# One core: a score block of the next quarter traced before the old quarter's last transpositions, and a routing with its sums in PSUM

## The chip, the core and the metric

The kernel runs on one core of a Trainium2 chip. The metric is device time in microseconds (us) of one execution, the lower the better. The engines are TensorE (PE in the rows), VectorE (DVE), ScalarE (ACT), GpSimd (POOL) and SyncE (SP, which issues most of the DMAs here); PEld is TensorE's loading of weights.

## What is computed

Three stages stand behind each other, all in fp32 accuracy.

1. Attention with random features, for 4 batches, 8 heads, 576 positions, 64 channels and 128 features. For q and k: `proj = x @ omega.T`, `h = proj - sum(x*x)/2`, `phi = exp(h - max(h))`. Then `kv = phi(k).T @ v`, `z = sum(phi(k))`, `out = phi(q) @ kv / (phi(q) @ z)`.
2. A mixture of 8 experts over the 2304 tokens of width 512: `logits = x @ w_gate`, the expert is the argmax of a row, its gate the softmax value there, and `y = gate * (max(x @ w1[e], 0) @ w2[e])`, with an inner width of 1024.
3. A dense layer: `h = x @ w_in` (512 to 2048), `g = h * sigmoid(1.702 h)`, `out = g @ w_out`.

## The kernel before, in words

**Attention in eight quarters.** A quarter is 4 heads of one batch, so two quarters make a batch. Each quarter has a q part (`qgen`) and a k part (`kgen`), which run beside each other: q of quarter i with k of quarter i + 1. The rows of a quarter are cut into five blocks, four of 128 x 512 score elements and one of half the width. A letter and the block's number say what is done:

- P: the score block (`ph_P`). TensorE makes `pr` (L344 in the first quarters, L350 and L351 with two fp16 halves later), VectorE reduces the maximum over features (L359, into a corner of the PSUM tile `small`), does two small operations with the squares sq (L368) and subtracts (L380), which gives `qp`. In k blocks of the first four quarters the subtraction is left to ScalarE's exponential (L376). `pr` has three buffers.
- X: TensorE transposes `qp` into `tq` (L430), ScalarE takes the exponential into `qpT` (L432).
- N: TensorE's products `num` (L444); VectorE adds the epsilon, inverts and scales into `xn` (L446 to L455).
- R: half of the quarter's `xn` is transposed for the experts: four 128-wide pieces into `tx` (L464) and a 64-wide rest into `small` (L466). ScalarE copies both as `xh` (L469), and VectorE makes the remainder `xl` (L473). There are two R per quarter, R0 and R1, and the corner of `small` for the rest exists once, so the second waits until the first was read.

The order of a quarter's steps is written out by hand in a string, and a list scheduler then orders the instructions of each engine by its own estimate, starting from the order in which the code is traced:

```python
W_Q = 17
W_K = 5
Q_ORDER = "P0 P1 X0 P4 X1 N0 P2 X4 N1 X2 P3 N4 X3 N2 R0 N3 R1"
```

Steps of q, of k and of the routing are merged by weights (17, 5 and 10). q and k of a quarter come by DMA into `m` (two buffers). ScalarE and GpSimd split them into fp16 halves `hl` (L307, L308), SyncE transposes these by DMA into `xT` (L309, three buffers), and GpSimd squares and folds `m` (L267, L272) for `sq` (L274). So the split of a later quarter's k stands on ScalarE among the exponentials and the copies `xh`.

**The routing of a batch** (`route_steps`) runs beside the following quarter. TensorE multiplies the gate weights' two halves with xh and xl into `lT_ps` (L529, L530), 16 rows: 8 experts, once for each half. ScalarE copies them as `lT`. Then come five transpositions into `lg_ps` (L537), two VectorE copies (L542, L543) and the sum of the two halves (L545), which is `lg`, tokens by experts. From it come the row maximum `rm`, the one-hot `oh`, `ex` for the softmax, the counts `ct_ps` by a product with ones (L561), the most frequent expert `es` (L565 to L571), and each token's expert number `ixf` (five `max`, five `max_index`, a cast: L588 to L591). SyncE loads `es` into a register (L604); only then can it issue the loads `st` of that expert's weights (L674), which ScalarE and VectorE or GpSimd split into `wh` and `wl` (L698, L700).

**The experts** (`m_ps`, `w_ps`, L136; `h1h` L732; `h1l` L735; `y` L783) are interleaved with attention as soon as routing 0 is done; until then attention runs alone:

```python
while 0 not in gate_t:
    done_a += next(A)
    tick()
```

Routing 3, the last, has attention behind it. Beside it run the last products of batch 2's experts and, on VectorE, the decoding `z` of output weights of the dense layer (L826 to L901). The dense layer follows (`qa` and others, L1146 and L1249).

Of the kernel before, what the change touches and what calls it, by code (L numbers as in the profile page):

```python
# [8 lines left out]
F32 = mybir.dt.float32  # L9
# [3 lines left out]
U32 = mybir.dt.uint32  # L13
I64 = mybir.dt.int64
ACTF = mybir.ActivationFunctionType
ALU = mybir.AluOpType
AX = mybir.AxisListType
# [5 lines left out]
def kernel(  # L23
# [13 lines left out]
    nc = tc.nc  # L37
    B, H, S, D = q.shape
    M = omega.shape[0]
    E, DM, F1 = w1.shape  # L40
    F2 = w_in.shape[1]
    NT = B * S
    P = 128
    T = 4
    TAIL = S - T * P
# [26 lines left out]
    W_Q = 17  # L72
    W_K = 5
    K_ORDER = (0, 1, 4, 2, 3)
    Q_ORDER = "P0 P1 X0 P4 X1 N0 P2 X4 N1 X2 P3 N4 X3 N2 R0 N3 R1"
    LAG_E = 2
    LAG_X = 1
    LAG_M = 0
# [27 lines left out]
    pp = ctx.enter_context(tc.tile_pool(name="pp", bufs=1, space=PSUM))  # L106
# [34 lines left out]
    ident = const.tile([P, P], F32, name="ident")  # L141
# [3 lines left out]
    iota8 = const.tile([P, E], F32, name="iota8")  # L145
# [26 lines left out]
    def setup_wg():  # L172
        nc.sync.dma_start(out=wg, in_=w_gate.rearrange("(k p) e -> p k e", p=P))
        nc.scalar.activation(out=wgs[:, :, 0], in_=wg, func=ACTF.Copy)
        nc.vector.tensor_tensor(out=wgs[:, :, 1], in0=wg, in1=f32(wgs[:, :, 0]), op=ALU.subtract)
# [7 lines left out]
    QB = H // QH  # L183
    NQ = B * QB
    asked = []
    clock = [0]
    late = []

# [107 lines left out]
    def halves_T(src, i, eng):  # L296
        sides[0] += 1
        if sides[0] <= FPX:
            return turned(src, i)
        if sides[0] - 1 in LO_DVE:  # L300
            eng = nc.vector
        m = src[i]
        hl = att.tile([P, NB, 2, D], F16, tag="hl", name="hl", bufs=2)
        xT = att.tile([P, NB, P], F16, tag="xT", name="xT", bufs=3)
        sq = att.tile([P, NB], F32, tag="sq", name="sq", bufs=3)
        for c in (slice(0, 8), slice(8, NB)) if i < FINE else (slice(0, NB),):
            nc.scalar.activation(out=hl[:, c, 0], in_=m[:, c], func=ACTF.Copy)  # L307
            eng.tensor_tensor(out=hl[:, c, 1], in0=m[:, c], in1=hl[:, c, 0], op=ALU.subtract)  # L308
            XQ.dma_start_transpose(out=xT[:, c], in_=hl[:, c].rearrange("p n a d -> p (n a d)"))  # L309
            square_sum(m, c, sq, FOLD_LATE)  # L310
        src[i] = (xT, sq, False)
# [102 lines left out]
    def qgen(i):  # L414
# [5 lines left out]
        src, kv = q_in.pop(i), kv_t.pop(i)  # L420
        xn = att.tile([P, T + 1, QH, D], F32, tag="xn", name="xn", bufs=1)
        xv = xn.rearrange("p t h d -> p t (h d)")
        qp, qt = {}, {}

        def X(i):
            w = 2 if i < 4 else 1
# [52 lines left out]

        for n, op in enumerate(Q_ORDER.split()):  # L480
            g = int(op[1])
            if op == "R0" and qd == 0:
                while x_done[0] < b - 1:
                    yield None
                xh_t[b] = (moe if b % 2 else xep).tile([P, KD, S], F32R, tag="xh", name="xh", bufs=1)
                xl_t[b] = (moe if b % 2 else xep).tile([P, KD, S], F32R, tag="xl", name="xl", bufs=1)
            if op[0] == "P":
                c = ph_P(i, src, qp, "qp", 3, g)
            else:
                c = {"X": X, "N": N, "R": XT}[op[0]](g)  # L490
            if n == 0 and i + 1 < NQ:
                load_v(i + 1)
            if n == KPRE and i + 2 < NQ:
                load_qk(k, k_in, i + 2, asked[-1] if i == QB + 1 else None)
                halves_T(k_in, i + 2, nc.vector if i + 2 < DVE_LO else nc.gpsimd)
            yield c
# [10 lines left out]


    gate_t, reg_t = {}, {}

    def route(b):
        g = route_steps(b)
# [7 lines left out]
    def route_steps(b):  # L520
# [10 lines left out]
            nc.scalar.activation(out=lT[:, c], in_=lT_ps, func=ACTF.Copy)  # L531
        yield 2.0
        yield 0
        lg_ps = pp.tile([P, T + 1, 2, E], F32, tag="n", name="lg_ps", bufs=1)
        for t in range(T + 1):
            n = P if t < T else TAIL
            nc.tensor.transpose(  # L537
                lg_ps[:n, t].rearrange("p a e -> p (a e)"), lT[:, t * P:t * P + n], ident[:2 * E, :2 * E]
            )
        lg2 = att.tile([P, T + 1, 2, E], F32, tag="lg2", name="lg2", bufs=1)  # L540
        nc.vector.memset(lg2[:, T], 0.0)
        nc.vector.tensor_copy(lg2[:, 0:T], lg_ps[:, 0:T])  # L542
        nc.vector.tensor_copy(lg2[:TAIL, T], lg_ps[:TAIL, T])  # L543
        lg = att.tile([P, T + 1, E], F32, tag="lg", name="lg", bufs=1)
        nc.vector.tensor_tensor(out=lg, in0=lg2[:, :, 0], in1=lg2[:, :, 1], op=ALU.add)  # L545


        rm = att.tile([P, T + 1, 1], F32, tag="rm", name="rm", bufs=2)
        nc.vector.tensor_reduce(out=rm, in_=lg, axis=AX.X, op=ALU.max)
# [32 lines left out]
                )  # L582
        cif = att.tile([P, 1], F32, tag="cif", name="cif", bufs=2)
        nc.vector.tensor_copy(cif, ci[:, 0:1])
        mx = att.tile([P, T + 1, 8], F32, tag="lmx", name="lmx", bufs=1)
        ix = att.tile([P, T + 1, 8], U32, tag="lix", name="lix", bufs=1)
        for t in range(T + 1):
            nc.vector.max(mx[:, t], lg[:, t])  # L588
            nc.vector.max_index(ix[:, t], mx[:, t], lg[:, t])
        ixf = att.tile([P, T + 1, 1], F32, tag="ixf", name="ixf", bufs=1)  # L590
        nc.vector.tensor_copy(ixf, ix[:, :, 0:1])  # L591
        eq = att.tile([P, T + 1, 1], F32, tag="eq", name="eq", bufs=1)
        nc.vector.tensor_scalar(out=eq, in0=ixf, scalar1=cif[:, 0:1], scalar2=None, op0=ALU.is_equal)
        nc.vector.memset(eq[TAIL:, T, :], 0.0)
# [405 lines left out]
    if True:  # L1000
# [6 lines left out]
        halves_T(q_in, 0, nc.vector if DVE_LO else nc.gpsimd)  # L1007
        load_qk(k, k_in, 1)
        setup_wg()
        halves_T(k_in, 1, nc.vector if DVE_LO else nc.gpsimd)  # L1010
        A, Mg = attention_gen(), moe_all()
        done_a = done_m = 0.0
# [14 lines left out]
        while a_live:  # L1027
            if force == "a" or (force is None and done_a - lead <= A_RATIO * done_m):
                c = next(A, "end")
# [515 lines left out]
```

## Time and profile before

| what | value |
|---|---|
| median of 3 runs | 767.19 us (766.09 to 768.16) |
| profiled execution | 767.65 us, of which its span 765.6 us |
| TensorE busy | 739.7 us (97%) |
| VectorE busy | 531.3 us (69%) |
| ScalarE busy | 338.6 us (44%) |
| GpSimd busy | 131.9 us (17%) |
| mean granted clock of TensorE | 0.99 |

The span is the time from the first to the last instruction; the execution's time holds some 2 us more. Busy shares are means over stages with different limits: where TensorE is full, the other engines' work lies beside it, and only where TensorE waits do they count. The granted clock is the share of TensorE's full speed.

### The profile page before, as it was taken

The numbers are of one execution on the slowest core, as the hardware profiler recorded it, in microseconds if no ns is written. First come the engines' busy times: TensorE is split into PE (matmuls) and PEld (weight loads), VectorE is DVE, ScalarE is ACT, GpSimd is POOL, SyncE is SP. The second block draws the span as 40 slices with busy tenths as digits, with TensorE's granted clock in tenths as the row PEclk, the third lists the DMA queues.
The fourth block names the chain that finished last, engine by engine and source line by source line (L and its number), as shares of the span: only waits on it lengthen the run. The fifth ranks groups of instructions, "written<-read, shape, count | busy, mean of one in ns | idle before, by whom it ended". The sixth has DMA issues, their size and how long they took to land.

```text
span 765.6 us, 14359 instructions
## 1 busy us (share of the span) xinstructions
PE 739.7 (97%) x5559; PEld 716.1 (94%) x5559; DVE 531.3 (69%) x1188; ACT 338.6 (44%) x638; POOL 131.9 (17%) x78
## 2 busy tenths in 40 slices
PE   7998799999999999989999999999999999999997
PEld 6877699999999999979999999999999999999996
DVE  5867867586776685556879559981368777777774
ACT  5554464335522332233427464554576433444331
POOL 3563377609500441000000000000000000000000
PEclk9999799999999999999999999999999999999999
DMA  5447594456725554198145558972978544443311
GB/s 157 117 131 187 123 302 97 120 140 193 189 60 162 150 179 134 51 234 287 59 161 197 177 171 295 316 263 100 332 273 298 172 138 138 137 129 117 115 29 32
DMA packets 136715, 127.57 MB, mean 167 GB/s; under 512 B 58176, under 2 KB 120896, under 8 KB 135744
## 3 DMA queue, kind: packets, MB, share of 16 engines
q1 hardware_dynamic: 123936, 98.85, 43.5%
q10 hardware_dynamic: 12704, 27.73, 10.3%
q8 instruction: 45, 0.74, 0.4%
q14 instruction: 30, 0.25, 0.1%
HBM read 79.68 MB, written 40.40 MB: 157 GB/s over the span
## 4 chain that ended last, share of the span: by engine, by line
PE 83%; DVE 8%; DMA 4%; issue 1%; ACT 1%; SPq 1%; POOL 0%; ACTq 0%; POOLq 0%; DVEq 0%
PE m_ps L136 19%; PE qa L1249 13%; PE qa L1146 13%; PE qm L1249 7%; PE w_ps L136 4%; PE pb L1249 3%; PE qm L1146 3%; PE qu L1146 3%; PE num L444 3%; PE kv_ps L402 3%; DMA st<-in_moe_w_dram 2%; PE qn L1146 2%; PE qt L1146 2%; PE tq L430 1%; PE pr L344 1%
## 5 line engine op out<-in xcount | busy, mean ns | idle before, releaser
L1146 PE MATMUL qa<-y,wi 128*128 128x384 f32 x576 | 109.2, 337 | 0.4 <-DVE g L901 0.4
L1146 PEld LDWEIGHTS qa<-y,wi 128*128 128x128 f32 x576 | 101.4, 188 | 0.8 <-DVE g L901 0.8
L136 PE MATMUL m_ps<-xh,wh 128*128 128x288 f32 x256 | 79.0, 309 | 4.1 <-DVE h1l L735 2.3
L136 PE MATMUL m_ps<-xh,wl 128*128 128x288 f32 x256 | 76.8, 300 | 0.1
L136 PE MATMUL m_ps<-xl,wh 128*128 128x288 f32 x256 | 76.4, 298 | 0.0
L700 POOL TENSOR_TENSOR wl<-st,wh 128x1024 fp32r<-128x1024 f32 x23 | 55.1, 2401 | 83.0 <-ACT wh L698 82.9
L359 DVE TENSOR_REDUCE small<-pr 128x4 f32<-128x512 f32 (+1 forms) x80 | 51.1, 639 | 11.8 <-PE pr L351 7.8
L698 ACT ACTIVATE wh<-st 128x1024 fp32r<-128x1024 f32 (+1 forms) x33 | 34.0, 1035 | 48.5 <-DMA st<-in_moe_w_dram 31.6
L136 PEld LDWEIGHTS m_ps<-xh,wh 128*128 128x128 f32 x256 | 48.6, 190 | 5.8 <-DVE h1l L735 3.6
L136 PE MATMUL m_ps<-h1h,wh 128*128 128x288 f32 x160 | 48.8, 305 | 0.9 <-DVE h1l L735 0.9
L136 PEld LDWEIGHTS m_ps<-xh,wl 128*128 128x128 f32 x256 | 48.6, 190 | 0.5 <-DVE wl L700 0.4
L735 DVE SCALAR_TENSOR_TENSOR h1l<-m_ps,h1h 128x288 fp32r<-128x288 f32 x64 | 28.9, 453 | 28.9 <-ACT h1h L732 28.8
L136 PEld LDWEIGHTS m_ps<-xl,wh 128*128 128x128 f32 x256 | 48.6, 190 | 0.0
L136 PE MATMUL m_ps<-h1l,wh 128*128 128x288 f32 x160 | 47.7, 298 | 0.0
L136 PE MATMUL m_ps<-h1h,wl 128*128 128x288 f32 x160 | 47.4, 298 | 0.0
L732 ACT ACTIVATE h1h<-m_ps 128x288 fp32r<-128x288 f32 x64 | 25.9, 407 | 48.5 <-PE m_ps L136 46.7
L1249 PE MATMUL qa<-p,p 128*128 128x256 f32 x360 | 46.2, 282 | 1.1 <-DVE p L855 0.8
L1249 PE MATMUL qa<-p,gs 128*128 128x256 f32 x360 | 45.9, 282 | 0.0
L1249 PEld LDWEIGHTS qa<-p,p 128*128 128x128 f32 x360 | 44.2, 189 | 1.6 <-DVE p L855 1.0
L1249 PEld LDWEIGHTS qa<-p,gs 128*128 128x128 f32 x360 | 44.2, 189 | 0.0
L444 PEld LDWEIGHTS num<-kv,qpT 128*128 128x128 f32 (+1 forms) x320 | 36.7, 184 | 5.4 <-ACT qpT L432 3.1
L444 PE MATMUL num<-kv,qpT 128*128 128x65 f32 (+1 forms) x320 | 39.3, 266 | 2.5 <-ACT qpT L432 1.4
(213 smaller groups left out, 1819.5 us busy)
## 6 DMA issues: line engine op xcount, KB each, us to landing
g_dram<-g ACTq DMA_DIRECT2D x48, 384.0 KB, 4.1
st<-in_moe_w_dram SPq DMA_DIRECT2D x31, 512.0 KB, 5.2
pg<-g_dram SPq DMA_DIRECT2D x10, 1024.0 KB, 5.7
raw<-in_moe_w_in_dram SPq DMA_DIRECT2D x16, 512.0 KB, 4.0
gt<-g_dram SPq DMA_DIRECT2D x8, 1024.0 KB, 5.4
p<-wo_dram SPq DMA_DIRECT2D x6, 1024.0 KB, 7.3
yt<-y_dram SPq DMA_DIRECT2D x12, 384.0 KB, 6.0
vm<-in_v_dram SPq DMA_DIRECT2D x32, 128.0 KB, 3.2
```

The lines of the kernel that those rows point to most:

```text
L136: ins = nc.tensor.matmul(out=ps, lhsT=a, rhs=b, start=start and n == 0, stop=stop and n == 2)
L344: nc.tensor.matmul(out=ps[:, :, h2], lhsT=xT[:, (2 * pr + h2) * 2 + t0 // 2], rhs=wbd)
L359: nc.vector.tensor_reduce(out=pm, in_=ps[:, :w], axis=AX.X, op=ALU.max, negate=on_act)
L402: nc.tensor.matmul(out=kv_ps[:, h, :], lhsT=kp[j // 2][:, j % 2, h2, :], rhs=vm[:, h, t, :], start=(t == 0), stop=False,)
L430: nc.tensor.transpose(tq[:, c, h2], qp[i][:, c, h2, :], ident)
L444: nc.tensor.matmul(out=ps[:n, c, h2, :], lhsT=lhsT, rhs=kv[:, h, :])
L698: nc.scalar.activation(out=hi[:, :, s], in_=st[:, :, s], func=ACTF.Copy)
L700: eng.tensor_tensor(out=lo[:, :, s], in0=st[:, :, s], in1=f32(hi)[:, :, s], op=ALU.subtract)
L732: nc.scalar.activation(out=hh[:, f], in_=ps, func=ACTF.Relu)
L735: nc.vector.scalar_tensor_tensor(out=hl[:, f], in0=ps, scalar=0.0, in1=f32(hh[:, f]), op0=ALU.max, op1=ALU.subtract)
L1146: ins = nc.tensor.matmul(out=ps, lhsT=w[:, a, ks], rhs=y[:, b, kk], start=start and kk + m == 0, stop=kk == 1 and m == 2, skip_group_check ...
L1249: ins = nc.tensor.matmul(out=ps, lhsT=x[:, f], rhs=w[i][:, f], start=start and f + m == 0, stop=f == NP - 1 and m == 2, skip_group_check=True,
```

## The change

Three edits. First, the string of steps gets an "F0" in front of R0: the next quarter's block P0 is traced there, and that quarter's own P0 then does nothing. Second, the logits' two halves are summed by TensorE: five fp32 products with a 16 x 8 matrix `fold` (two identities on top of each other) take the place of the five transpositions, so that the copies are half as wide and the sum falls away; `lg` is now one tile for all batches. Third, the expert numbers come from the one-hot: it is multiplied by 8 minus the expert's number (`left`), the row maximum is taken, and 8 minus it is the number of the first expert that has the maximum. Two constants are set up at the start.

```diff
-    Q_ORDER = "P0 P1 X0 P4 X1 N0 P2 X4 N1 X2 P3 N4 X3 N2 R0 N3 R1"
+    Q_ORDER = "P0 P1 X0 P4 X1 N0 P2 X4 N1 X2 P3 N4 X3 N2 F0 R0 N3 R1"
...
+    first = {}
...
-        qp, qt = {}, {}
+        qp, qt = first.pop(i, {}), {}
...
             if op[0] == "P":
-                c = ph_P(i, src, qp, "qp", 3, g)
+                c = 0 if g in qp else ph_P(i, src, qp, "qp", 3, g)
+            elif op[0] == "F":
+                c = ph_P(i + 1, q_in[i + 1], first.setdefault(i + 1, {}), "qp", 3, g) if i + 1 < NQ else 0
...
+    lg = att.tile([P, T + 1, E], F32, name="lg")
+    lgx = att.tile([P, 2, E], F32, name="lgx")
+    fold, left = lgx[:2 * E, 0], lgx[:, 1]
+
+    def setup_route():
+        nc.gpsimd.memset(lg[:, T], 0.0)
+        nc.vector.tensor_tensor(out=fold, in0=ident[:2 * E, 0:E], in1=ident[:2 * E, E:2 * E], op=ALU.add)
+        nc.vector.tensor_scalar(out=left, in0=iota8, scalar1=-1.0, scalar2=float(E), op0=ALU.mult, op1=ALU.add)
...
-        lg_ps = pp.tile([P, T + 1, 2, E], F32, tag="n", name="lg_ps", bufs=1)
+        lg_ps = pp.tile([P, T + 1, E], F32, tag="n", name="lg_ps", bufs=1)
         for t in range(T + 1):
             n = P if t < T else TAIL
-            nc.tensor.transpose(
-                lg_ps[:n, t].rearrange("p a e -> p (a e)"), lT[:, t * P:t * P + n], ident[:2 * E, :2 * E]
-            )
-        lg2 = att.tile([P, T + 1, 2, E], F32, tag="lg2", name="lg2", bufs=1)
-        nc.vector.memset(lg2[:, T], 0.0)
-        nc.vector.tensor_copy(lg2[:, 0:T], lg_ps[:, 0:T])
-        nc.vector.tensor_copy(lg2[:TAIL, T], lg_ps[:TAIL, T])
-        lg = att.tile([P, T + 1, E], F32, tag="lg", name="lg", bufs=1)
-        nc.vector.tensor_tensor(out=lg, in0=lg2[:, :, 0], in1=lg2[:, :, 1], op=ALU.add)
-
+            nc.tensor.matmul(out=lg_ps[:n, t], lhsT=lT[:, t * P:t * P + n], rhs=fold)
+        nc.vector.tensor_copy(lg[:, 0:T], lg_ps[:, 0:T])
+        nc.vector.tensor_copy(lg[:TAIL, T], lg_ps[:TAIL, T])
...
-        mx = att.tile([P, T + 1, 8], F32, tag="lmx", name="lmx", bufs=1)
-        ix = att.tile([P, T + 1, 8], U32, tag="lix", name="lix", bufs=1)
-        for t in range(T + 1):
-            nc.vector.max(mx[:, t], lg[:, t])
-            nc.vector.max_index(ix[:, t], mx[:, t], lg[:, t])
         ixf = att.tile([P, T + 1, 1], F32, tag="ixf", name="ixf", bufs=1)
-        nc.vector.tensor_copy(ixf, ix[:, :, 0:1])
+        nc.vector.tensor_tensor(out=oh, in0=oh, in1=left.unsqueeze(1).to_broadcast([P, T + 1, E]), op=ALU.mult)
+        nc.vector.tensor_reduce(out=ixf, in_=oh, axis=AX.X, op=ALU.max)
+        nc.vector.tensor_scalar(out=ixf, in0=ixf, scalar1=-1.0, scalar2=float(E), op0=ALU.mult, op1=ALU.add)
```

Line numbers of the changed kernel lie one higher up to the routing, and 11 to 1 higher behind it. The scheduler moves more than the diff says; three places follow.

On VectorE, at the seam of quarters 1 and 2, before (numbers tell the buffers apart; pr_876 is the first block of quarter 2, pr_897 a block of k):

```order
L274 TENSOR_REDUCE sq_867<-m_861 128x18
L473 TENSOR_TENSOR xl_547<-small_130,xh_546 128x64
L473 TENSOR_TENSOR xl_547<-tx_826,xh_546 128x512
L473 TENSOR_TENSOR xl_547<-small_130,xh_546 128x64
L359 TENSOR_REDUCE small_130<-pr_876 128x4
L368 TENSOR_TENSOR small_130<-small_130,sq_608 128x4
L368 TENSOR_TENSOR mx_885<-small_130,sq_608 128x4
L380 TENSOR_TENSOR qp_889<-pr_876,mx_885 128x512
L359 TENSOR_REDUCE small_130<-pr_897 128x4
```

And of the change, where pr_812 is the first block of quarter 2 and pr_902 that block of k:

```order
L360 TENSOR_REDUCE small_130<-pr_812 128x4
L275 TENSOR_REDUCE sq_887<-m_881 128x18
L369 TENSOR_TENSOR small_130<-small_130,sq_622 128x4
L369 TENSOR_TENSOR mx_821<-small_130,sq_622 128x4
L381 TENSOR_TENSOR qp_825<-pr_812,mx_821 128x512
L474 TENSOR_TENSOR xl_561<-tx_846,xh_560 128x512
L474 TENSOR_TENSOR xl_561<-small_130,xh_560 128x64 x2
L360 TENSOR_REDUCE small_130<-pr_902 128x4
```

The block of quarter 2 (a reduce, two small operations, a subtraction) has moved from behind the three xl to in front of them, and the two xl of the 64-wide rests now come last. At the seam of quarters 0 and 1 it moves in the same way.

On TensorE, in front of the gate products of routing 0, before (the first row is the second 64-wide transposition of quarter 1, then a score block of quarter 2):

```order
L466 MATMUL small_130<-ident_79,xn_616 128x64
L350 LDWEIGHTS xT_607
L350 MATMUL pr_915<-wh2_117,xT_607 128x128
L351 LDWEIGHTS xT_607
L351 MATMUL pr_915<-wl2_118,xT_607 128x128
...
L529 MATMUL lT_ps_941<-xh_546,wgs_96 16x288
L530 MATMUL lT_ps_941<-xl_547,wgs_96 16x288
L529 MATMUL lT_ps_941<-xh_546,wgs_96 16x288
L530 MATMUL lT_ps_941<-xl_547,wgs_96 16x288
```

And of the change:

```order
L352 MATMUL pr_963<-wl2_118,xT_621 128x128
L540 MATMUL lT_ps_946<-xh_560,wgs_96 16x288
L541 MATMUL lT_ps_946<-xl_561,wgs_96 16x288
L540 MATMUL lT_ps_946<-xh_560,wgs_96 16x288
L541 MATMUL lT_ps_946<-xl_561,wgs_96 16x288
L540 MATMUL lT_ps_946<-xh_560,wgs_96 16x288
L467 MATMUL small_130<-ident_79,xn_630 128x64
L541 MATMUL lT_ps_946<-xl_561,wgs_96 16x288
L540 MATMUL lT_ps_936<-xh_560,wgs_96 16x288
```

The 64-wide transposition has moved from in front of the gate products to behind the fifth of them, and a further score block (pr_963) to in front of them. At the seam of quarters 0 and 1 the second such transposition has moved behind the first tq of the new quarter, and on ScalarE its copy xh behind that quarter's first qpT. The count product ct_ps of routing 0, which stood in front of the last k block, now stands behind it, behind the transpositions of block 3 and behind the first score block of quarter 3.

On VectorE, from the counts of routing 3 to es, before (z is the decoding of output weights, h1l the experts'):

```order
L565 TENSOR_REDUCE ct_3878<-ct_ps_3876 128x8
L602 COPY rr_3915<-gate_3886 128x5
L835 SCALAR_TENSOR_TENSOR z_233<-raw_o_234,z_233 128x512
L826 TENSOR_SCALAR z_233<-raw_o_234 128x512
L568 MAX cm_3880<-ct_3878 128x8
L901 TENSOR_TENSOR z_233<-z_233 128x256
L831 SCALAR_TENSOR_TENSOR z_233<-raw_o_234,z_233 128x512
L569 MAX_INDEX ci_3881<-cm_3880,ct_3878 128x8
L735 SCALAR_TENSOR_TENSOR h1l_4318<-m_ps_4358,h1h_4317 128x288
L835 SCALAR_TENSOR_TENSOR z_233<-raw_o_234,z_233 128x512
L571 CAST es_3884<-ci_3881 128x1
```

And of the change:

```order
L603 COPY rr_3871<-gate_3852 128x5
L902 TENSOR_TENSOR z_238<-z_238 128x256 x2
L569 TENSOR_REDUCE ct_3844<-ct_ps_3842 128x8
L590 TENSOR_TENSOR oh_3833<-oh_3833,lgx_132 128x40
L572 MAX cm_3846<-ct_3844 128x8
L591 TENSOR_REDUCE ixf_3864<-oh_3833 128x5
L573 MAX_INDEX ci_3847<-cm_3846,ct_3844 128x8
L592 TENSOR_SCALAR ixf_3864<-ixf_3864 128x5
L736 SCALAR_TENSOR_TENSOR h1l_4271<-m_ps_4272,h1h_4270 128x288
L575 CAST es_3850<-ci_3847 128x1
```

The full-width pieces of z (L826, L831, L835) have gone from between the two, half-width ones (L901, now L902) stand ahead, and the three operations for ixf stand in between.

TensorE, ScalarE, GpSimd and SyncE otherwise hold the same instructions; TensorE's order is the same from about 320 us on.

## Rows read from the trace of the kernel before

**Rows 1.** The page, part 1: busy us, share of the span, instructions.

```profile
PE 739.7 (97%) x5559; PEld 716.1 (94%) x5559; DVE 531.3 (69%) x1188; ACT 338.6 (44%) x638; POOL 131.9 (17%) x78
```

**Rows 2.** Stretches of 20 us: length, busy us by engine, granted clock, DMA.

```profile
100.00:120.00 20.00, 20.00 (x176) 19.61 (x175) 14.25 (x39) 13.60 (x22) 16.89 (x9) 1.00 0.72 209
...
300.00:320.00 20.00, 20.00 (x152) 18.82 (x151) 7.84 (x40) 3.46 (x9) 0.00 (x0) 1.00 0.17 57
```

**Rows 3.** VectorE's timeline, 40 to 66 us: start, duration, what, [idle before].

```profile
45.07 0.23 DVE L473 TENSOR_TENSOR xl<-small,xh 128x64 fp32r<-128x64 f32 x1 [3.36 <-ACT xh L469]
...
46.42 0.70 DVE L359 TENSOR_REDUCE small<-pr 128x4 f32<-128x512 f32 x1
...
48.16 0.69 DVE L359 TENSOR_REDUCE small<-pr 128x4 f32<-128x512 f32 x1
...
55.72 0.16 DVE L446 TENSOR_SCALAR rd<-num 128x4 f32<-128x4 f32 x1 [1.57 <-PE num L444]
```

**Rows 4.** TensorE's timeline of the same stretch.

```profile
46.07 1.08 PE L344 MATMUL pr<-wbd,xT 128*128 128x256 f32 x4
48.30 0.66 PE L430 MATMUL tq<-ident,qp 128*128 128x128 f32 x4 [1.15 <-DVE qp L380]
```

**Rows 5.** The chain that ended last, 60 to 96 us: start, duration, what.

```profile
70.63 0.70 DVE xl L473
...
71.68 0.13 PE lT_ps L530
...
78.25 0.38 PE lg_ps L537 x5
...
88.35 0.06 DVE es L571
...
89.22 4.37 DMA st<-in_moe_w_dram
```

**Rows 6.** TensorE's timeline, 73 to 96 us.

```profile
82.29 1.08 PE L430 MATMUL tq<-ident,qp 128*128 128x128 f32 x4 [0.35 <-DVE qp L380]
83.17 0.31 PE L350 MATMUL pr<-wh,xT 128*128 128x128 f16 x1
83.28 0.31 PE L351 MATMUL pr<-wl,xT 128*128 128x128 f16 x1
...
94.30 0.40 PE L136 MATMUL m_ps<-xh,wh 128*128 128x288 f32 x1 [1.73 <-ACT wh L698]
```

**Rows 7.** VectorE's timeline, 64.5 to 92.5 us.

```profile
71.24 0.21 DVE L473 TENSOR_TENSOR xl<-small,xh 128x64 fp32r<-128x64 f32 x1
...
79.90 1.35 DVE L545 TENSOR_TENSOR lg<-lg 128x40 f32<-128x40 f32 x1
...
82.39 0.33 DVE L551 TENSOR_TENSOR oh<-lg,rm 128x40 f32<-128x40 f32 x1
...
88.26 0.15 DVE L571 CAST es<-ci 128x1 int32<-128x1 uint32 x1
```

**Rows 8.** The chain, 296 to 362 us.

```profile
301.50 0.84 PE num L444 x8
...
316.84 0.35 DVE lmx L588 x4
...
317.73 0.70 DVE lix L589 x5
...
323.67 0.07 DVE es L571
```

**Rows 9.** Waits, 296 to 400 us: us in total, times, longest.

```profile
PE m_ps L136 <- DVE h1l L735: 3.0, 4, 0.9
```

**Rows 10.** Stretches of 4 us, columns as in rows 2.

```profile
80.00:84.00 4.00, 3.64 (x28) 3.31 (x28) 3.92 (x25) 1.09 (x4) 2.58 (x2) 0.62 0.24 55
```

**Rows 11.** GpSimd's timeline, 74 to 96 us.

```profile
79.08 2.11 POOL L267 TENSOR_TENSOR m<-m 128x1152 f32<-128x1152 f32 x1
81.27 1.39 POOL L272 TENSOR_TENSOR m<-m 128x576 f32<-128x576 f32 x1
```

More of the change, by code (lines that the diff above doesn't have):

```diff
@@ L1009 @@
         setup_wg()
+        setup_route()
         halves_T(k_in, 1, nc.vector if DVE_LO else nc.gpsimd)
```

## Prediction

> **What bounds the kernel now.** The first view is the page's table of engines: TensorE is busy for 739.7 of 765.6 us [rows 1], so whatever the change does elsewhere, only some 26 us in which TensorE stands still can be won, and TensorE work that is added counts in full wherever TensorE is full. The second view is the table by stretches: in 100 to 120 us and in 300 to 320 us TensorE has no gap at all [rows 2]. Work on VectorE is free there. The change must therefore be read where TensorE waits: in the first 100 us (attention alone, then the first routing) and behind the last routing.
>
> The third view is VectorE's timeline at the seam of quarters 0 and 1. It sits idle for 3.36 us in front of xl, because ScalarE's copy xh is late, and only then does the new quarter's first score block follow: its reduce starts at 46.42, the next block's at 48.16 [rows 3]. TensorE meanwhile waits 1.15 us at 48.30 for that block's result qp [rows 4]. The fourth view, the chain that ended last between 60 and 96 us, goes from xl (70.63) over the gate products lT_ps and the logits to es (88.35), and from es over the first expert weights' load (4.37 us) [rows 5] to the first expert product at 94.30, which had waited 1.73 us for the weights [rows 6]. From es to that product it is always the same: 94.30 − 88.26 = 6.04 us (es begins at 88.26 by the timeline [rows 7]; the chain enters it at 88.35), a load and a split that the change doesn't touch. Behind the last routing the same chain from es (323.67) over the weights reaches TensorE; there it waits for h1l four times, 3.0 us in all [rows 8, 9].
>
> **The change, part by part.** The sum is made against the profiled execution, 767.65 us (span 765.6 and 2.05 around it). It lies 0.46 above the median of the runs, 767.19; that is taken off at the end.
>
> *Seam 0 to 1 (first score block moved): −1.0, between 0 and −1.75.* The block takes 48.16 − 46.42 = 1.74 us of VectorE [rows 3]. It now stands in front of xl, in the 3.36 us gap; its products are at their old place on TensorE, at about 40 us, so it finds them ready. Not all of the 1.74 arrives. The order on TensorE puts the second 64-wide transposition of xn (into small) behind the new quarter's first tq, and ScalarE puts its copy xh behind qpT. VectorE works in order, so its last xl, and the whole new quarter behind it, waits for that. Worked out from the rows: the next block's products, begun at 46.07, last until about 46.8; tq takes 0.66 [rows 4]; ScalarE's qpT, its copy xh and xl are an estimate of 1.0 together: about 48.4. The next block's reduce would start no earlier than the 48.16 of before. What is won is on TensorE and ScalarE: tq no longer waits 1.15 us for qp. VectorE later stands idle 1.57 us at 55.72, waiting for a product num that hangs on that tq [rows 3]; from there on VectorE is the one that is full, up to the load that the second seam's xl waits for. So up to 1.6 us of the gain reaches that load, and an exponential of a k block, now in TensorE's way for a score buffer, takes a part back: 1.0.
>
> *From xl to es of routing 0: −0.2, between −1.5 and +1.2.* VectorE loses, by the rows: the first block, 1.74 (as above); the addition, 1.35 [rows 7]; five indices 0.70 and five maxima, 0.35 for four [rows 8], with the cast about 1.2. It gains one more k block in front of es (a block without its last subtraction, about 1.2 as an estimate) and three small operations (about 0.35). That is −2.7. Four waits stand against it. (1) The second small transposition stands behind five gate products now (0.13 each [rows 5]); transposition, xh and xl follow one another, so the last xl ends at about 72.65 where it ended at 71.45 (71.24 + 0.21 [rows 7]): +1.2. (2) ScalarE runs an exponential and the split of q ahead of qpT, so num is late: +0.2. (3) The count product ct_ps stands behind the transpositions of block 3 and the first block of quarter 3. At the clock granted there, 0.62 in 80 to 84 us [rows 10], the four transpositions take 1.08 and the eight score products, 0.11 apart, 0.9 [rows 6], with ct_ps some 2.4; VectorE has an estimated 1.4 us of other work until it needs the counts. So 1.0 at that clock and about 0 at the full one; the clock changes within the stage, and half is taken: +0.5. (4) The new one-hot comes about 0.5 us earlier than the old one, into GpSimd's fold, which runs from 81.27 to 82.66 [rows 11]. The old addition began at 79.90 and took 1.35 us, ending as GpSimd's square of 79.08 ended (2.11 long); the old one-hot, begun 0.27 before the fold ended, took 0.33 [rows 7, 11]. So +0.6, between 0 and 1.39.
>
> The Trainium skill, in "SBUF — State Buffer", section "Who interferes with whom", says that a VectorE instruction with two inputs in SBUF and a GpSimd instruction that reads SBUF exclude each other, the one issued later waiting for the whole of the other. The trace agrees, with the addition's 1.35 us; by the rule alone the one-hot could wait for the whole fold, 1.4 in place of 0.6, and the sum would be 0.8 higher.
>
> Where es comes earlier or later, the first expert product does by as much, and TensorE's order holds about the same work in front of it as before (four score products more, two num fewer).
>
> *The products of the logits: +1.1, between +0.5 and +2.0.* Five transpositions took 0.38 us, 0.076 each [rows 5]. The five products of full fp32 are two passes each, as num's are (four written, eight in the row). Ten passes at the transpositions' 0.076 are 0.76: +0.38. At num's 0.105 (eight in 0.84 us [rows 8]) it is +0.67, at 0.055, half of the score products' 0.11 at the low clock [rows 6], +0.17. The nearest are the transpositions, with the same stationary columns of lT. Three of the four routings run where TensorE is full: 3 × 0.38.
>
> *Routing 3: −1.8, between −0.5 and −3.0.* Its logits stand some 14 products earlier on TensorE, the indices, maxima and the addition are gone (0.70 + 0.44 [rows 8] and a sum, against 0.35 that is new), and the full-width decode pieces lie ahead of the logits now and not between them and es; four half-width ones come in. ct's product, about 36 products behind the logits, then sets es, at 320 to 321 in place of 323.67. Three us earlier, the weights' splits stand ready when TensorE comes: of the 3.0 us of waits for h1l [rows 9], in which VectorE held h1l back behind a split, all but those that hang on TensorE's own freeing of a buffer should go.
>
> *Row numbers, constants, seams 2 to 7: 0.* The two constants are made in the first 20 us on VectorE and GpSimd, beside loads. In routings 1 and 2 TensorE hides the saved VectorE work; if it weren't full there, some 2.5 us each could show.
>
> Sum: −1.0 − 0.2 + 1.1 − 1.8 = −1.9, so 765.75 for such an execution, **765.3** on the median's footing.
>
> **The rivals.** *All gains arrive.* No second small transposition is in the way and ct doesn't wait: −1.75 − 1.5 + 0.5 − 3.0 = −5.75, at the most 761.4; half-way from the forecast, 763.3. For it: 3.36 us of gap; against it: the order shows the transposition moved. *The stall only moves.* The last xl waits for as long as was saved at both seams, es of routing 0 is 0.5 later, and routing 3 brings 0.5: 0 + 0.5 + 1.1 − 0.5 = +1.1, so 768.3. For it: 48.4 against 48.16. *Slower: the clock.* In 80 to 84 us TensorE was granted 0.62, with 3.64 of 4 us busy [rows 10]. If the new waits between 70 and 90 us keep the level of 1.2 GHz into the full stretch behind 94.30, each busy us there costs about 0.38; with ct's other 0.5 us, 12 us of it make 5.1, −1.9 + 5.1 = +3.2, so 770.4. It decides from 4.2 us, about 10 us of full work at that level. Against it: by 100 us the grant was 1.00 [rows 2].
>
> **How the numbers follow.** A measurement tells about 0.3%, 2.3 us, from no change: faster is below 764.9, slower above 769.5. The forecast has 0.47 (763.6 to 767.0 by the terms' nearer bounds, 0.20 of it below 764.9), all gains 0.19, the stall moved 0.21, the clock 0.13 (nearly all above 769.5). Faster 0.39, same 0.47, slower 0.14. The range, 761.9 to 769.4, leaves out the clock case and the far end of all gains.
>
> **What would show it.** In the new profile: the gap before xl at the first seam with a block in it, and a new one between the two last xl; no 1.15 us wait of tq; the load at the second seam about 1 us earlier; es of routing 0 within 1 us of the second seam's xl plus 17.7; an lg product group of 0.7 to 1.1 us; es of routing 3 before 321.5 and fewer waits for h1l behind it. The prediction is wrong if es of routing 0 moves by over 2 us either way, or if routing 3's earlier es leaves the 3.0 us standing.

## The result, and the profile after

The changed kernel takes **776.88 us** (median; 774.06 to 780.83), 1.0121 times the kernel before (95% interval 1.0091 to 1.0152). It is slower, and the time lies outside the predicted range. The execution profiled took 779.28 us, of which 777.5 are its span, 11.9 more than before's 765.6. The page of the changed kernel, part 1:

```profile
PE 744.5 (96%) x5579; PEld 721.9 (93%) x5579; DVE 526.5 (68%) x1130; ACT 338.4 (44%) x638; POOL 132.0 (17%) x79
```

Against [rows 1] VectorE has 4.8 us less to do, as meant, and TensorE is busy for 4.8 us more; the rest of the 11.9 is TensorE standing still, 777.5 − 744.5 = 33.0 in place of 25.9 us. The prediction looked at the first 100 us and behind the last routing, and took TensorE to be full in between. TensorE's timeline of the changed kernel, all of its waits of over 1.5 us between 40 and 400 us:

```profile
50.68 1.13 PE L345 MATMUL pr<-wbd,xT 128*128 128x256 f32 x4 [1.70 <-DVE small L369]
...
70.83 0.42 PE L540 MATMUL lT_ps<-xh,wgs 128*16 128x288 f32 x1 [1.83 <-DVE xl L474]
...
96.59 0.61 PE L136 MATMUL m_ps<-xh,wh 128*128 128x288 f32 x1 [3.25 <-ACT wh L699]
...
192.50 0.66 PE L431 MATMUL tq<-ident,qp 128*128 128x128 f32 x4 [1.59 <-DVE xl L474]
...
291.31 0.40 PE L136 MATMUL m_ps<-xh,wh 128*128 128x288 f32 x1 [2.11 <-DVE y L784]
...
343.30 0.51 PE L136 MATMUL w_ps<-h1h,wh 128*128 128x288 f32 x1 [3.73 <-ACT h1h L733]
```

The last three stand in stretches that had no such wait before: between 100 and 400 us the longest wait of TensorE was then 0.93 us. What follows each is in the stretches of the changed kernel (columns as in [rows 2]):

```profile
180.00:200.00 20.00, 18.41 (x156) 17.88 (x155) 12.34 (x39) 10.55 (x16) 15.80 (x8) 0.91 0.64 176
280.00:300.00 20.00, 17.89 (x134) 17.46 (x133) 15.77 (x36) 6.86 (x11) 7.56 (x3) 0.91 0.52 174
340.00:360.00 20.00, 16.70 (x113) 16.63 (x114) 12.30 (x22) 6.37 (x10) 0.00 (x0) 0.91 0.55 159
...
193.30:196.70 3.40, 3.40 (x26) 3.40 (x24) 2.99 (x8) 3.24 (x6) 3.40 (x3) 0.50 0.72 200
...
292.20:295.60 3.40, 3.40 (x18) 3.40 (x17) 2.92 (x9) 1.36 (x2) 0.32 (x1) 0.51 0.93 325
...
343.40:346.80 3.40, 3.40 (x14) 3.33 (x15) 3.40 (x8) 0.15 (x1) 0.00 (x0) 0.51 0.46 150
```

Within 1 us of the end of each of the three waits TensorE is granted 0.50, the lower level (1.2 GHz), for 3.4 us in which it has work throughout. So each of these waits cost itself and about 3.4 × 0.5 = 1.7 us of slow work: 1.59 + 2.11 + 3.73 and 3 × 1.7 are 12.5 us. The same three stretches of the kernel before:

```profile
180.00:200.00 20.00, 20.00 (x191) 19.45 (x190) 16.37 (x49) 10.97 (x19) 18.82 (x10) 1.00 0.77 209
280.00:300.00 20.00, 19.61 (x152) 18.44 (x151) 16.42 (x37) 7.11 (x15) 6.62 (x3) 1.00 0.49 162
340.00:360.00 20.00, 18.27 (x133) 17.41 (x132) 12.91 (x22) 8.04 (x13) 0.00 (x0) 1.00 0.79 256
```

The 12.5 us aren't the whole loss, and not all of them are a loss against before, which stood still in the last of these stretches too. Where the 11.9 us arise is seen when the same products of TensorE are set beside each other in the two profiles. The changed kernel is 1.5 us ahead at the attention products kv_ps of the second seam (62.79 for 64.27), 2.3 behind at the first expert product (96.59 for 94.30), 3.2 behind at the kv_ps in front of the wait at 192.5 (186.33 for 183.16), 6.4 at the next ones (220.17 for 213.79), 7.5 at those of 262.19 (254.73 before) and 12.2 at the first product of the dense layer (412.60 for 400.39), which keeps that to its end. So the changed kernel was behind by 3.2 us in front of the first of the three waits.

Why TensorE waits is read from the chain that ended last (start, duration, what) of the changed kernel, in three pieces:

```profile
64.81 3.39 DMA m<-in_k_dram
...
70.09 0.70 DVE xl L474
...
71.25 0.24 PE lT_ps L541
...
81.33 1.20 PE lg_ps L548 x10
...
89.98 5.90 DMA st<-in_moe_w_dram
...
180.48 6.10 DMA m<-in_q_dram
...
186.68 1.16 ACT hl L308
187.84 0.12 ACT xh L470
...
191.78 0.68 DVE xl L474
...
330.07 0.06 DVE es L575
...
331.37 10.42 DMA st<-in_moe_w_dram
...
342.95 0.31 ACT h1h L733
```

At 192.5 it is a queue of four. The last piece of q's load was late, and ScalarE's split hl waited for that load; the copy xh, next in ScalarE's order, waited with it, and VectorE's xl at 187.99 waited for xh. Behind that xl stand 3.5 us of VectorE's work, mostly score blocks, and then the wide xl (191.78) that tq waited for. Why the load was late stands in SyncE's queue (start, duration, what) of the changed kernel:

```profile
177.74 0.36 SPq L610 DMA_DIRECT2D r_dram<-rr  x1
...
179.60 0.83 SPq L791 DMA_DIRECT2D y_dram<-y  x2
180.48 0.68 SPq L259 DMA_DIRECT2D m<-in_q_dram  x1
```

The load stands behind a store of the row numbers rr and stores of y, which wait for VectorE. It does so in the kernel before as well; its SyncE queue:

```profile
173.27 1.01 SPq L790 DMA_DIRECT2D y_dram<-y  x2
174.33 2.08 SPq L258 DMA_DIRECT2D m<-in_q_dram  x2
```

So the load was not moved behind the stores; the queue came 6.2 us later, where TensorE was 3.2 us later. VectorE's timeline of the changed kernel has what the stores wait for, and the rows that answer to [rows 3] and [rows 7]:

```profile
48.06 0.23 DVE L474 TENSOR_TENSOR xl<-small,xh 128x64 fp32r<-128x64 f32 x1 [1.55 <-ACT xh L470]
48.32 0.70 DVE L360 TENSOR_REDUCE small<-pr 128x4 f32<-128x512 f32 x1
...
72.81 0.23 DVE L474 TENSOR_TENSOR xl<-small,xh 128x64 fp32r<-128x64 f32 x1 [1.90 <-ACT xh L470]
...
83.91 0.19 DVE L555 TENSOR_TENSOR oh<-lg,rm 128x40 f32<-128x40 f32 x1
...
89.13 0.13 DVE L575 CAST es<-ci 128x1 int32<-128x1 uint32 x1
...
174.06 1.47 DVE L594 TENSOR_SCALAR eq<-ixf,cif 128x5 f32<-128x5 f32 x1
176.67 1.04 DVE L597 SCALAR_TENSOR_TENSOR rr<-eq,ixf 128x5 f32<-128x5 f32 x1
...
177.81 1.40 DVE L602 TENSOR_TENSOR total<-total,hit 128x1 f32<-128x1 f32 x1
...
187.99 0.23 DVE L474 TENSOR_TENSOR xl<-small,xh 128x64 fp32r<-128x64 f32 x1 [4.79 <-ACT xh L470]
...
283.48 0.68 DVE L832 SCALAR_TENSOR_TENSOR z<-raw_o,z 128x512 int32<-128x512 int32 x1
284.42 2.87 DVE L836 SCALAR_TENSOR_TENSOR z<-raw_o,z 128x512 int32<-128x512 int32 x1
...
290.82 0.44 DVE L784 TENSOR_TENSOR y<-m_ps,gb 128x288 f32<-128x288 f32 x1
```

VectorE's timeline of the kernel before:

```profile
169.03 0.22 DVE L593 TENSOR_SCALAR eq<-ixf,cif 128x5 f32<-128x5 f32 x1
```

And GpSimd's timeline of the changed kernel:

```profile
173.10 2.40 POOL L309 TENSOR_TENSOR hl<-m,hl 128x1152 f16<-128x1152 f32 x1 [21.65 <-ACT hl L308]
...
284.37 5.17 POOL L701 TENSOR_TENSOR wl<-st,wh 128x1024 fp32r<-128x1024 f32 x2 [9.25 <-ACT wh L699]
```

Three small operations, of five, five and one elements on each partition, took 1.47, 1.04 and 1.40 us while GpSimd worked. Before, the same three took 0.22, 0.15 and 0.16, ahead of GpSimd's work that began at 173.28. In the changed kernel the count product of this routing came 3.4 us later (169.23 for 165.88), its es 5.2 later (173.80 for 168.55; it stands behind an h1l that waited for ScalarE), and so these three came into GpSimd's work, and y and its store behind them. Likewise a z of 0.68 took 2.87 while GpSimd's wl ran. The second wait, at 291.31, is y standing behind such z on VectorE. The Trainium skill, "SBUF — State Buffer", section "Who interferes with whom", says that a VectorE instruction with two inputs in SBUF and a GpSimd instruction that reads SBUF exclude each other; the 2.87 against 0.68 us of z agree. Before there are such long z as well (one of 2.50 us at 287.32), but no y that TensorE wanted stood behind them. What differs is who is queued there.

The third wait, at 343.30, is the load of the last expert's weights: 10.42 us.

### The profile page after: what moved, and what is told of

Same layout as the page of the kernel before. It is cut to its first block, busy times and chain, and to the rows that moved or that the text cites. A ratio compares the mean times of both kernels' runs of the same rounds, so it can differ in the third digit from the quotient of the medians.

```text
span 777.5 us, 14348 instructions
## 1 busy us (share of the span) xinstructions
PE 744.5 (96%) x5579; PEld 721.9 (93%) x5579; DVE 526.5 (68%) x1130; ACT 338.4 (44%) x638; POOL 132.0 (17%) x79
## 4 chain that ended last, share of the span: by engine, by line
PE 84%; DVE 6%; DMA 5%; ACT 2%; issue 1%; SPq 1%; ACTq 0%; DVEq 0%
PE m_ps L136 18%; PE qa L1251 13%; PE qa L1148 13%; PE qm L1251 7%; PE w_ps L136 4%; PE pb L1251 3%; PE qm L1148 3%; PE qu L1148 3%; PE num L445 3%; DMA st<-in_moe_w_dram 3%; PE kv_ps L403 3%; PE pr L345 2%; PE tq L431 2%; DMA m<-in_q_dram 2%; PE qn L1148 2%; PE qt L1148 1%
## 5 line engine op out<-in xcount | busy, mean ns | idle before, releaser
L136 PE MATMUL m_ps<-xl,wh 128*128 128x288 f32 x256 | 77.2, 302 | 0.0
L136 PE MATMUL m_ps<-h1l,wh 128*128 128x288 f32 x160 | 48.4, 302 | 0.0
```

The costliest lines, as they stand in the source:

```text
L136: ins = nc.tensor.matmul(out=ps, lhsT=a, rhs=b, start=start and n == 0, stop=stop and n == 2)
```

## The experiments

The prediction's theory allowed itself no loss in the middle. Four explanations were put against each other: the moved block loses (A), the routing's edits lose, by the products of the logits (B, P), the list scheduler's new order loses whatever the edit (C), and one or another wait found above is the cause (D, S). Ratios are to the kernel before.

**The parts alone.** First the moved block, without the routing's edits (all lines of the diff with `first` and F0):

```diff
-    Q_ORDER = "P0 P1 X0 P4 X1 N0 P2 X4 N1 X2 P3 N4 X3 N2 R0 N3 R1"
+    Q_ORDER = "P0 P1 X0 P4 X1 N0 P2 X4 N1 X2 P3 N4 X3 N2 F0 R0 N3 R1"
```

> The kernel before with the first edit alone: the next quarter's first score block is traced in front of the transpositions, the routing is the old one. Theory A, the seams: the block stands in front of the last copies xl, TensorE waits at the seams and runs at the lower clock after each wait; then nearly all of the loss is here, 773 to 778 us. Theory B, the routing: the products and the row numbers make the weights late; then this one is at 764 to 768. Theory C, the order: the old order was a lucky one and any edit that lets the scheduler order anew loses; then this and the next three all lie at 770 or above.

Measured 766.64, ratio 1.0013 (0.9985 to 1.0041): A falls, and with it C as it stands here, that any new order loses. Then the changed kernel with the string of before, that is without F0:

> The changed kernel without the moved block: products into PSUM and row numbers from the one-hot stay. Theory A (seams): 765 to 768, with no wait of over 1 us at the seams of the middle. Theory B (routing): 773 to 778. Theory C (any new order): 770 or above.

Measured 769.95, 1.0040 (1.0019 to 1.0061), below what B gave. Against the 767.04 of the kernel before beside these runs the two parts are −0.4 and +2.9 us; they don't add up to 10.2. The products of the logits alone, with `max` and `max_index` kept:

```diff
-            nc.tensor.transpose(
-                lg_ps[:n, t].rearrange("p a e -> p (a e)"), lT[:, t * P:t * P + n], ident[:2 * E, :2 * E]
-            )
+            nc.tensor.matmul(out=lg_ps[:n, t], lhsT=lT[:, t * P:t * P + n], rhs=fold)
```

> The products into PSUM alone; the row numbers by max and max_index as before. By the forecast's term the three full routings pay +1.1 us and the first one gains about 1: 766 to 768. Theory A: the same. Theory B: if the products are the costly half, 772 or above. Theory C: 770 or above.

Measured 775.55, 1.0103 (1.0071 to 1.0135), more than all routing edits together. Its profile shows that the loss doesn't need a long wait: between 100 and 400 us TensorE has none over 1.22 us. But behind its waits of 1.11 us at 178.19 and of 1.22 at 341.47 (with one of 0.67 at 342.80) the grant is 0.50 as well (180.1 to 183.5 and 343.9 to 347.3). The row numbers from the one-hot alone:

```diff
-            nc.vector.max(mx[:, t], lg[:, t])
-            nc.vector.max_index(ix[:, t], mx[:, t], lg[:, t])
...
+        nc.vector.tensor_reduce(out=ixf, in_=oh, axis=AX.X, op=ALU.max)
```

> The row numbers from the one-hot alone; transpositions and their sum as before. Theory A: 765 to 767, es of the first routing earlier by about 0.8 us. Theory B: if the row numbers are the costly half, 772 or above. Theory C: 770 or above.

Measured 769.07, 1.0027 (1.0009 to 1.0046). And the changed kernel with the transpositions and the sum of before, so F0 and the row numbers:

> The moved block and the row numbers, with the old transpositions and their sum. Theory P: 765 to 768, the loss is gone with the products. Theory C: the products' own time is gone, about 2.4 to 3.2 us (0.81 us more for each of the routings), and the rest is another draw: 766 to 774.

Measured 777.39, 1.0117 (1.0075 to 1.0159): without the products the kernel is as slow, so P falls. The parts neither add up nor follow what each does: adding an edit that saves work turns 766.6 into 777.4.

**Another order with nothing edited.** One merging weight, that of the routing's steps, is 11 in place of 10, in the kernel before and in the changed one; every operation stays.

```diff
-    ROUTE_N = 10
+    ROUTE_N = 11
```

> The kernel before with not one operation changed: only the weight with which the routing's steps are merged goes from 10 to 11, and the scheduler orders anew. Theory C, the order: the loss of the changed kernel lies in which instructions happen to stand behind which in the engines' orders; then this one loses as well, 769 to 776 us, by waits of TensorE of over 1 us that the kernel before doesn't have, each with a stretch of half clock behind it. Theory P, the products: what costs is the products and what hangs on them; then this one is the kernel before, 766 to 768.

> The changed kernel with the same weight of 11, all three edits in. Theory C: another draw, and since the changed kernel's is a poor one, more likely better: 769 to 775, with other waits than those at 192, 291 and 343 us. Theory P: 775 to 779, the same as the changed kernel.

Measured 773.49, 1.0103 (1.0067 to 1.0138), and 779.25, 1.0182 (1.0122 to 1.0241). The kernel before loses 1% by its order alone, so C holds in this: an order by itself can cost that much. For the changed kernel C expected a better draw, 769 to 775, and was wrong. The profiled execution of the kernel before with the weight 11 took 769.73, below its median, and shows the mechanism of 192.5 at another place. The chain of the kernel before with the weight 11:

```profile
115.96 4.00 DMA m<-in_q_dram
...
120.06 1.16 ACT hl L307
121.22 0.49 ACT qpT L432
```

Here the copy behind the split that waits for q's load is qpT; TensorE's timeline has the wait of 4.09 us; with the weight 10 TensorE is busy from 100 to 200 us without a gap ([rows 2], and 80.00 of 80.00 from 120 on):

```profile
121.76 0.44 PE L430 MATMUL tq<-ident,qp 128*128 128x128 f32 x2 [4.09 <-ACT qpT L432]
```

**The decoding put later.** The wait of 2.11 us at 291 stands behind z, so the decoding of the output weights begins at step 275 in place of 245: in the changed kernel, and then in the kernel before.

```diff
-    OUT_FROM = 245
+    OUT_FROM = 275
```

> The changed kernel with the decoding of the output weights started later (the clock tick from which it may run goes from 245 to 275); TensorE's order is the same for the first half of the program. The wait of 2.1 us at 291 us, for y behind a decoding piece that took 2.87 us in place of 0.68, and the 1.7 us lost at half clock behind it should go: Theory C 772 to 774, or less if the wait at 343 goes too. Theory P: no change, 776 to 778.

> The control for the late decoding: the kernel before with the decoding from tick 275 and nothing else. Theory D, the decoding is always in the way: this gains as much as the changed kernel did, some 4 to 5 us, 762 to 764. Theory C, order: the kernel before has no wait of TensorE on y at that place to lose, so it gains nothing, and a new draw costs 0 to 6 us: 766 to 773.

Measured 771.98, 1.0064 (1.0040 to 1.0088), and 775.96, 1.0114 (1.0075 to 1.0154). The changed kernel gains 4.9. Its stretches and TensorE's timeline there:

```profile
280.00:300.00 20.00, 20.00 (x165) 19.65 (x164) 14.28 (x38) 8.21 (x13) 10.03 (x4) 1.00 0.26 80
340.00:360.00 20.00, 17.60 (x131) 17.14 (x130) 12.23 (x20) 7.86 (x12) 0.00 (x0) 1.00 0.83 280
```

```profile
193.30 0.66 PE L431 MATMUL tq<-ident,qp 128*128 128x128 f32 x4 [0.79 <-DVE xl L474]
```

The waits of 2.11 and 3.73 us are gone and so are the stretches at 0.50: this ties the loss to these waits. But they went together, and at 193 too something moved that lies before any decoding, so this is a redraw as well. The kernel before loses 9.3 by the same line, more than C allowed it, so D, decoding that is simply in the way, falls. TensorE's timeline of the kernel before with late decoding:

```profile
330.74 0.40 PE L136 MATMUL m_ps<-xh,wh 128*128 128x288 f32 x1 [2.52 <-DVE h1l L735]
```

**The moved block at some seams only.** The changed kernel with F0 at the two first seams, whose gap it was meant for, and with F0 at the later ones only; the second condition is `2 <= i < NQ - 1`:

```diff
-                c = ph_P(i + 1, ...) if i + 1 < NQ else 0
+                c = ph_P(i + 1, ...) if i < 2 else 0
```

> The changed kernel with the block moved at the first two seams alone (quarters 0 to 1 and 1 to 2); the order is the changed kernel's until about 85 us. Theory S, the moved block hurts at the seams where TensorE was full: 768 to 771, the products' 2.4 to 3.2 us alone. Theory C: a new draw behind the second seam, 769 to 778, and the waits on xl near 190 us come back or not without regard to the block.

> The other half: the block moved from the third seam on alone. Theory S: 774 to 778, the loss is here. Theory C: 769 to 778, not told apart from the one before by its seams but by which waits of over 1 us it has; each such wait and the half clock behind it should account for the difference to the routing alone (770 us).

Measured 780.84, 1.0190 (1.0153 to 1.0226), and 774.93, 1.0100 (1.0048 to 1.0152). S, that the block costs at the full seams, falls: leaving it out there is slower, and also slower than C's 778. TensorE waits elsewhere in the first of the two, by its timeline:

```profile
339.40 0.58 PE L136 MATMUL m_ps<-xh,wh 128*128 128x288 f32 x1 [4.38 <-DVE h1l L736]
```

**The moved block with late decoding.** The block alone cost nothing, and the late decoding had helped one kernel:

> The moved block alone (766.6 us) with the late decoding, as a version that might beat both kernels. Theory D: 762 to 764. Theory C: 766 to 772; a draw that comes out below 765 isn't excluded, since the block alone has 2.0 us of waits between 240 and 260 us and 1.5 us at 322 to lose.

Measured **764.17**, 0.9970 (0.9953 to 0.9987), the only one below both kernels. Its profiled execution took 762.79 and has between 100 and 400 us no wait of TensorE longer than 1.00 us (the kernel before: 0.93). That it lies 11.8 below the kernel before with late decoding, where the same block made no difference with early decoding, fits an effect of the order; it is the best of several draws, not a price of the block.

**What the edits cost beside the order.** Three more neutral changes of a weight, each in the kernel before and in the changed one: ROUTE_N 9, ROUTE_N 12, and the weight of q's steps 18 in place of 17.

```diff
-    W_Q = 17
+    W_Q = 18
```

> The kernel before with the routing's weight 9 for 10, a further draw of its order. Theory C (the order given is a good draw, and the edits themselves cost only the products): 768 to 776, about as far above 767 as the other two draws of its operations, 773.5 and 776.0. Theory E (the edits themselves cost most of the 10 us): 765 to 769.

> The changed kernel with the same weight 9. Theory C: 2 to 4 us above what draws of the kernel before give on the mean, 770 to 780. Theory E: 8 to 12 above its partner with the same weight.

> The kernel before with the routing's weight 12. Theory C: 768 to 776. Theory E: 765 to 769.

> The changed kernel with weight 12. Theory C: 770 to 780, 2 to 4 above the mean of the draws of before. Theory E: 8 to 12 above its partner.

> The kernel before with the weight of the q steps 18 for 17. Theory C: 768 to 776. Theory E: 765 to 769.

> The changed kernel with the weight of the q steps 18. Theory C: 770 to 780, 2 to 4 above the mean of the draws of before. Theory E: 8 to 12 above its partner.

All pairs, the medians in us:

| order | before | changed | difference |
|---|---|---|---|
| as given | 766.64 (beside the changed kernel) | 776.88 | +10.2 |
| ROUTE_N 9 | 769.77 | 775.50 | +5.7 |
| ROUTE_N 11 | 773.49 | 779.25 | +5.8 |
| ROUTE_N 12 | 777.40 | 783.34 | +5.9 |
| W_Q 18 | 778.72 | 785.99 | +7.3 |
| OUT_FROM 275 | 775.96 | 771.98 | −4.0 |
| mean of the five redraws | 775.07 | 779.21 | +4.1 |

Each line was run beside kernels before of its own, whose medians lie between 766.63 and 768.02. The five differences give +4.1 with an interval of −1.6 to 9.8 (standard deviation 4.6, five values); without the decoding's pair, whose change isn't neutral for z, the four lie at 5.7 to 7.3, above C's 2 to 4 and below E's 8 to 12. C's ranges were missed upwards by both kernels with ROUTE_N 12 and W_Q 18. The redrawn kernel before has waits of the same kind; TensorE's timeline with the weight 18:

```profile
362.18 1.09 PE L136 MATMUL w_ps<-h1h,wh 128*128 128x288 f32 x3 [2.42 <-ACT h1h L732]
```

So the 10.2 us between 766.64 and 776.88 come apart in this way: the kernel before lies 775.07 − 766.64 = 8.4 below its own redraws; the changed one lies 779.21 − 776.88 = 2.3 below its own; and 4.1 are between the two sets: 8.4 − 2.3 + 4.1 = 10.2. With the four neutral pairs alone it is 8.2 − 4.1 + 6.2. In both the kernel before lies some 8 us below its redraws, so its order is a good one; whether the 10.2 are more order or more edits isn't settled. That the edits cost all 8 to 12 us isn't borne out; that they cost nothing isn't excluded. Nor are the weights pure chance: in both kernels the time rises from ROUTE_N 10 to 12, so a larger weight may cost something of its own.

The profiles say what the edits' share consists of. TensorE stands still for 25.9 us (span less busy time) in the kernel before and for 29.0 to 36.1 in its five redraws; for 33.0 in the changed kernel and for 29.6 to 38.3 in its redraws. If each busy microsecond is weighed with the clock granted in it, nine profiles without the products of the logits have 731.3 to 733.2 us of work for TensorE, 732.6 in the mean, and the ten with them 733.9 to 736.9, 735.3 in the mean. So the products cost some 2.7 us wherever they stand; what else lies between two of these kernels is waiting and low clock.

## Why the prediction was wrong

**The step that failed** is "Row numbers, constants, seams 2 to 7: 0", with the assumption behind it that TensorE hides all that changes between 100 and 300 us. It hides saved VectorE work. It doesn't hide work that comes late or is queued anew: 1.59 us at 192.5 and 2.11 at 291.3 are new waits in that stretch, each with 1.7 us of half-speed work behind it, 7.1 in all. The prediction priced the operations that its two or three places showed moving, and neither the many that the scheduler moved elsewhere nor a first stage that ends later. Other orders of the same operations differ by up to 12 us, more than every term of the sum. Neither of the prediction's two signs of being wrong appeared: es of routing 0 moved by 0.9, and the waits for h1l went.

**The products of the logits, "+1.1, between +0.5 and +2.0".** The place was right, the size wrong: ten passes take 1.20 us (81.33 in the chain of the changed kernel), not 0.76, so 0.12 a pass, above even num's 0.105. Against 0.38 that is +0.82 a routing, +2.5 for the three in full stretches, beyond the bound of 2.0. The transpositions, chosen as the nearest row, were the wrong neighbour.

**Seam 0 to 1, "−1.0".** The mechanism was right as far as TensorE (1.5 us ahead at the kv_ps of 62.79), but the gain went no further. The last xl came at 48.06 and the next reduce at 48.32, where 48.4 was worked out, and tq's 1.15 us wait of [rows 4] is gone. But k's load, whose arrival the second seam's xl waits for, began at 64.81 and the first xl behind it at 70.09; before, these were 64.79 and 70.14: the 1.0 us never arrived there. TensorE's new wait, 1.70 us at 50.68 for VectorE's small operations, stands in place of the one removed. That is the rival in which the stall only moves, at this place.

**From xl to es of routing 0, "−0.2".** The last xl ended at 73.04 (72.65 worked out), and the one-hot took 0.19 without meeting GpSimd, so the 0.6 kept for that was saved. Still es began at 89.13, 0.9 later than 88.26 [rows 7], inside the bound of +1.2. "From es to that product it is always the same", 6.04 us, was false: 96.59 − 89.13 = 7.46, since the load took 5.90 us in place of 4.37 [rows 5]. So the first expert product came 2.3 later, 0.9 by es and 1.4 behind it. Why the load was slower stayed open.

**Routing 3, "−1.8".** The waits for h1l went as forecast, but not the way it was forecast. The waits of the changed kernel between 296 and 410 us:

```profile
PE w_ps L136 <- ACT h1h L733: 4.1, 2, 3.7
...
PE m_ps L136 <- DVE h1l L736: 0.7, 1, 0.7
```

Of the 3.0 us for h1l [rows 9] 0.7 are left. But es itself, forecast at 320 to 321, came at 330.1, since the whole stage had slipped, and the weights that it asks for took 10.42 us; TensorE then waited 3.73 for h1h behind their split. That an earlier es would have removed the waits for h1l is therefore not shown.

**The clock.** The rival named the clock, at 70 to 90 us, and part of it came: around the new wait of 1.83 us at 70.83 TensorE is granted 0.50 from 70.4 to 77.2, and the gate products take 0.24 us each, against 0.13 before [rows 5]. The last of them begins at 75.02 in place of 73.24. But before has low stretches of its own from 50.2 on, and the first 120 us have the same mean grant, 0.94, in both. What is new is the low clock behind 100 us. No length of wait tells when the grant falls: here it fell behind waits of 1.59 us, in the kernel with the products alone behind 1.11, and not behind 1.70 us at 50.68.

The accounts of the 11.9 us of the span can be closed with it. TensorE stands still 7.1 us more. Of the 4.8 us more of busy time some 3.9 are the clock: TensorE works 20.7 us at the lower level in place of 12.9, and half of the difference is lost. The remaining 0.9 stands where four times 0.82 for products was to be expected; single profiles scatter by 2 to 3 us in this, and the means above gave 2.7.

**What stays open:** why the first expert load is slower, and with it the first part of the lateness; which edit moves y behind z; why before's order is a good one; why loads of the same size take 4.4, 5.9 or 10.4 us; what decides whether the grant falls behind a wait; and whether the edits cost more than the products' 2.7 to 3.3, since the sets differ by 4.1 or 6.2.

## What to carry to other kernels

Where a list scheduler orders the queues, an edit is two things, its own work and a new order of everything behind it, and at a TensorE share of 97% the second can be the larger: here 12 us between orders of the same operations, against some 3 us of work. So before an effect of 1% is credited to an edit, draw the order of both kernels anew a few times (a merging weight one higher and lower) and compare the sets. In the trace, look at what stands in front of the operations that TensorE waits for: a copy behind a split that waits for a load on ScalarE, a load behind stores on SyncE that wait for VectorE, a result behind VectorE work that GpSimd blocks. Such a queue may have stood there before without harm; what counts is whether its work now comes late.

## What the hardware showed

- Waits of 1.59, 2.11 and 3.73 us in TensorE's full stretches were each followed by some 3.4 us at a granted 0.50. That isn't so of every wait: with the block at the late seams only, a wait of 2.11 us at 291.48, for the same y, left the grant at 1.00, and so did one of 1.55 us at 189 in the kernel before with the weight 11; with the products alone a wait of 1.11 us at 178.19 was followed by 3.4 us at 0.50.
- Counted by the granted clock, TensorE's work in nineteen profiles of these kernels agrees within 2 us (without the products) and 3 us (with them), while its busy time ranges from 734.1 to 746.3.
- An fp32 product of 16 x 128 by 16 x 8 appears as two rows of 0.12 us: five take 1.20 us, where five transpositions of the same columns take 0.38.
- VectorE operations of five, five and one elements on each partition took 1.47, 1.04 and 1.40 us beside GpSimd's work, ending with GpSimd's operation (175.50, 177.69 and 179.19); ahead of it they took 0.22, 0.15 and 0.16.
